# The first batch's attention as one hand-written list, with weight conversions at a fixed pace

## The chip, the cores and the metric

The program runs on one core of a Trainium2 chip. Its engines are TensorE (PE; PEld is its weight load), VectorE (DVE), ScalarE (ACT), GpSimd (POOL) and SyncE (SP), which issues nearly all transfers. The metric is the device time of one execution in microseconds.

## What is computed

Nystrom attention over 8 batches of 8 heads (576 tokens, 64 wide), and two feed-forward layers behind it:

```python
q_lm = q.reshape(B, H, 32, 18, 64).mean(axis=3)        # landmarks; k_lm the same
A, Bm, C = sm(q, k_lm), sm(q_lm, k_lm), sm(q_lm, k)    # sm: scaled softmax
Z = Bm.T / (norm1(Bm) * norminf(Bm) + 1e-6)
for _ in range(6): Z = 2 * Z - Z @ Bm @ Z
x = (A @ Z @ C @ v)                                    # 4608 x 512
x = relu(x @ w_in) ** 2 @ w_out                        # w_in 512 x 2048
...                                                    # then top-1 of 8 experts, 512 x 1024 x 512
```

The two layers' weights w_in and w_out arrive as 64-bit floats and are turned into 32-bit floats on the chip. A product is kept exact enough by splitting each operand in a high and a low part and summing three products.

## The kernel before

**Stages.** A *prologue* does batch 0's attention and converts the first weights. Then, for each batch b, `gemm(b)` makes two passes c = 0, 1 over 288 tokens each. A pass runs over 16 slices f of the hidden width: six matmuls make `hp` from `gb` (the product G of the attention's small factor `wt` with w_in, in rounds n of 512 columns, rows 4n to 4n+3 of f) and `ab` (the transposed A); ACT makes `r` (relu) and `gh`, `g2` (squares), DVE `gl`; twelve matmuls of `second` add the slice to four banks `acc` with w_out's parts `wo`, two slices later. From batch 1 on, G is made from the converted w_in that has been written to memory (`win_d`) and is read back as `wi`. The attention of batch b+1 is a generator of steps (`unit`); `point`, four times a slice, takes steps at `RATES[b, c]`. After batch 7 the experts' stage follows.

**Conversion.** `convert` handles 32 pieces of 128 x 512, first the 16 of w_in, then the 16 of w_out: a transfer `raw` (four buffers), a cast of the high half (`m`, on ACT or POOL), a scaled copy of the low half (`r`, ACT), and two additions on POOL (`halves`) into `wf` (w_in) or `w` (w_out). `wo` takes a high part (ACT) and a low part (DVE). In the prologue pieces are taken by a count (`CONV_SOON`, `CONV`), later on four of five ticks.

**What sets the order.** The framework's list scheduler places the instructions of each engine from priorities (`high_priority`) and dependencies; `follow(a, b)` ties a behind b. In the prologue the attention's steps have high priority, and `sooner` gives a further one to the chain that ends in `wt`: landmarks, softmax of B (`mb`, `bc`), its powers (`ee`, `ef`, six rounds of a matmul and a copy), values, `wz`, `wt`. Beside it runs A: scores, exponentials (`aa`), `at`, `ab`. Win_d's stores and the loads of batch 1's q and k go out in the prologue as buffers come free.

## Time and profile before

| | us |
|---|---|
| median of 3 runs | 1259.39 (1259.34 to 1260.92) |
| profiled execution | 1259.2 |
| its span in the trace | 1257.5 |
| PE busy | 1206.7 (96%) |
| ACT, DVE, POOL busy | 615.2, 591.3, 421.3 |
| mean granted TensorE clock | 0.978 of full |

The span is what the trace covers, from the first instruction to the last. A busy PE is one with a matmul in flight; its clock has two levels, 1.2 and 2.4 GHz, and the granted clock of a stretch is the mean share of the upper one.

### The profile page before, as it was taken

The numbers are of one execution on the slowest core, as the hardware profiler recorded it, in microseconds if no ns is written. First come the engines' busy times: TensorE is split into PE (matmuls) and PEld (weight loads), VectorE is DVE, ScalarE is ACT, GpSimd is POOL, SyncE is SP. The second block draws the span as 40 slices with busy tenths as digits, with TensorE's granted clock in tenths as the row PEclk, the third lists the DMA queues.
The fourth block names the chain that finished last, engine by engine and source line by source line (L and its number), as shares of the span: only waits on it lengthen the run. The fifth ranks groups of instructions, "written<-read, shape, count | busy, mean of one in ns | idle before, by whom it ended". The sixth has DMA issues, their size and how long they took to land.

```text
span 1257.5 us, 25149 instructions
## 1 busy us (share of the span) xinstructions
PE 1206.7 (96%) x9834; PEld 1078.6 (86%) x9834; DVE 591.3 (47%) x1498; ACT 615.2 (49%) x1433; POOL 421.3 (34%) x568
## 2 busy tenths in 40 slices
PE   4598999999999999999999999999999999999996
PEld 3377888989989989989989999998888888888885
DVE  5586466567547557556556332233333323323231
ACT  5586364564564564564564454553343433424331
POOL 5787514332233233232112000163342423424220
PEclk7699999999999999999999999999999999999998
DMA  9944333252152142141133210152534435343231
GB/s 339 336 164 135 124 122 109 91 168 61 59 171 64 53 158 77 53 158 58 54 120 108 69 37 2 39 151 84 143 105 139 129 115 159 108 125 110 90 96 40
DMA packets 88408, 142.24 MB, mean 113 GB/s; under 512 B 6430, under 2 KB 61758, under 8 KB 84702
## 3 DMA queue, kind: packets, MB, share of 16 engines
q1 hardware_dynamic: 87854, 139.97, 34.4%
q8 instruction: 79, 1.29, 0.4%
q0 software_dynamic: 288, 0.43, 0.1%
q14 instruction: 43, 0.35, 0.1%
q10 hardware_dynamic: 144, 0.20, 0.0%
HBM read 117.47 MB, written 23.11 MB: 112 GB/s over the span
## 4 chain that ended last, share of the span: by engine, by line
PE 90%; DVE 3%; DMA 3%; ACT 2%; POOL 1%; issue 1%; SPq 0%; POOLq 0%; ACTq 0%; DVEq 0%
PE acc L402 32%; PE hp L402 32%; PE y L402 17%; PE two L398 4%; PE bank L398 2%; PE bank L410 1%; DMA raw<-in_moe_w_in_dram 1%; PE pl L398 1%; DMA v<-in_v_dram 1%; PE pt L1168 1%; DVE x L488 1%; DMA t<-in_q_dram 1%; DVE gl L1079 1%; ACT r L185 0%; DVE ma L559 0%
## 5 line engine op out<-in xcount | busy, mean ns | idle before, releaser
L402 PE MATMUL acc<-gh,wo 128*128 128x288 f32 x2048 | 453.5, 299 | 7.7 <-ACT wo L218 5.0
L402 PEld LDWEIGHTS acc<-gh,wo 128*128 128x128 f32 x2048 | 341.1, 189 | 30.0 <-ACT gh L1077 8.4
L402 PE MATMUL acc<-gl,wo 128*128 128x288 f32 x1024 | 288.9, 298 | 1.1 <-DVE gl L1079 1.1
L402 PE MATMUL hp<-ab,gb 128*128 128x288 f32 x1536 | 255.7, 301 | 1.6 <-ACT r L1076 1.5
L402 PEld LDWEIGHTS hp<-ab,gb 128*128 128x128 f32 x1536 | 216.0, 189 | 21.3 <-issue 11.8
L1076 ACT ACTIVATE r<-hp 128x288 f32<-128x288 f32 x256 | 105.4, 412 | 256.0 <-PE hp L402 254.4
L1079 DVE TENSOR_TENSOR gl<-g,gh 128x288 fp32r<-128x288 f32 x256 | 131.4, 514 | 198.8 <-ACT g L1078 192.6
L402 PE MATMUL y<-s,h 128*128 128x512 f32 (+1 forms) x896 | 223.0, 396 | 0.8 <-ACT h L1311 0.5
L402 PEld LDWEIGHTS hp<-xs,s 128*128 128x128 f32 x1536 | 212.2, 188 | 7.5 <-DVE ls L1522 0.3
L402 PE MATMUL hp<-xs,s 128*128 128x288 f32 x1536 | 217.1, 295 | 0.2 <-DVE ls L1522 0.2
L402 PEld LDWEIGHTS acc<-gl,wo 128*128 128x128 f32 x1024 | 193.4, 189 | 4.0 <-DVE gl L1079 3.0
L402 PEld LDWEIGHTS y<-s,h 128*128 128x128 f32 (+1 forms) x896 | 160.6, 184 | 37.7 <-ACT h L1311 0.7
L230 POOL TENSOR_TENSOR s<-r,s 128x256 fp32r<-128x256 f32 x128 | 102.0, 819 | 234.8 <-ACT s L218 234.8
L1311 ACT ACTIVATE h<-hp 128x288 fp32r<-128x288 f32 x128 | 52.6, 412 | 186.8 <-PE hp L402 172.6
L1314 DVE SCALAR_TENSOR_TENSOR h<-hp,h 128x64 fp32r<-128x64 f32 (+2 forms) x192 | 62.6, 354 | 166.3 <-ACT h L1311 165.9
L1077 ACT ACTIVATE gh<-r 128x288 fp32r<-128x288 f32 x256 | 114.2, 446 | 12.5 <-PE acc L402 5.8
L1078 ACT ACTIVATE g<-r 128x288 f32<-128x288 f32 x256 | 110.6, 432 | 5.3 <-DVE gl L1079 5.0
L218 ACT CAST s<-r 128x512 fp32r<-128x512 f32 x128 | 77.6, 617 | 71.4 <-PE y L402 56.1
L499 POOL COPY x<-x 32x576 f32<-32x576 f32 x48 | 33.9, 706 | 195.7 <-DVE x L488 102.7
L224 DVE TENSOR_TENSOR s<-r,s 128x512 fp32r<-128x512 f32 x64 | 50.9, 795 | 103.3 <-ACT s L218 103.3
L230 POOL TENSOR_TENSOR xs<-xr,xs 128x576 fp32r<-128x576 f32 x32 | 45.9, 1459 | 64.0 <-ACT xs L218 48.0
L444 POOL TENSOR_TENSOR st<-t 128x288 f32<-128x288 f32 x50 | 40.7, 835 | 75.1 <-DMA t<-in_q_dram 73.1
(198 smaller groups left out, 1097.7 us busy)
## 6 DMA issues: line engine op xcount, KB each, us to landing
r<-in_moe_w_dram SPq DMA_DIRECT2D x128, 256.0 KB
wi<-win SPq DMA_DIRECT2D x28, 1024.0 KB
t<-in_k_dram SPq DMA_DIRECT2D x16, 576.0 KB
t<-in_q_dram SPq DMA_DIRECT2D x16, 576.0 KB
v<-in_v_dram SPq DMA_DIRECT2D x32, 288.0 KB
x_d<-x SPq DMA_DIRECT2D x16, 576.0 KB
xr<-x_d SPq DMA_DIRECT2D x16, 576.0 KB
raw<-in_moe_w_in_dram SPq DMA_DIRECT2D x16, 511.8 KB
```

The costliest lines, as they stand in the source:

```text
L218: hi = self.nc.scalar.copy(out=t[:, 0], in_=raw)
L224: lo_eng.tensor_tensor(out=t[:, 1], in0=raw, in1=t[:, 0].bitcast(F32), op=ALU.subtract)
L230: self.nc.gpsimd.tensor_tensor(out=out[:, p], in0=in0[:, p], in1=in1[:, p], op=op)
L398: self.in_run(lambda: self.nc.tensor.matmul(out, **kw))
L402: mm = self.nc.tensor.matmul(out, **kw)
L444: add = lambda out, in0, in1: self.nc.gpsimd.tensor_tensor(out=out, in0=in0, in1=in1, op=ALU.add)
L1076: nc.scalar.activation(out=r, in_=hp[:, 0:HC], func=ACTF.Relu)
L1077: nc.scalar.activation(out=gh, in_=r, func=ACTF.Square)
L1078: nc.scalar.activation(out=g2, in_=r, func=ACTF.Square)
L1079: nc.vector.tensor_tensor(out=gl, in0=g2, in1=gh.bitcast(F32), op=ALU.subtract)
L1311: nc.scalar.activation(out=h[:, t0:t1], in_=hp[:, 0:HC], func=ACTF.Relu)
L1314: nc.vector.scalar_tensor_tensor(out=h[:, to + a:to + z], in0=hp[:, a - t0:z - t0], scalar=0.0, in1=h[:, a:z].bitcast(F32), op0=ALU.max, o ...
```

## The change

The generator of batch 0's attention gives way to one list in `prologue`. While `strict` is true, the wrapper `Lanes` ties each instruction behind the one that was written before it on the same engine, SP's transfers too. This lasts until rounds 0 and 1 of G are out. The list interleaves the attention with `cv()`, a step of the conversion. Three pieces of w_out follow the first eight of w_in, then both alternate. In the list, odd pieces from 5 on are cast on ACT and the rest on POOL; afterwards odd ones on POOL and even ones on DVE. In the pass (0, 0) each slice takes two steps of conversion (`CONV = 2.0`), releases two held stores of w_in and, at three slices, sums of batch 1's landmarks. Rounds 2 and 3 of G come at slices 6 and 10. DVE takes over one of the squares in that pass, all sums of batch 0 and 1, and batch 0's half of the products with 1/sum. Batch 1's loads and stores into `win_d` move behind the list, its attention steps come slower, and its G rounds later (`G_LATER`).

```diff
-CONV_BUFS = 2
+CONV_BUFS = 3
+CONV = 2.0
+SUMS_AT = {3: ("k", 0), 5: ("k", 1), 7: ("q", 0)}
+OUT_AHEAD = 3
+FIRST_G = (6, 10)
-RATES = {(0, 0): 0.3, (0, 1): 0.8}
+RATES = {(0, 0): 0.2, (0, 1): 0.65}
-G_STEPS = {7: 0, 10: 1, 13: 2, 15: 3}
+G_STEPS = {(1, 7): 0, (1, 10): 1, (1, 13): 2, (1, 15): 3}
+G_LATER = {(1, 15): 0, (2, 2): 1, (2, 6): 2, (2, 10): 3}
...
+    def in_lane(self, name, op):
+        if self.strict is not None and hasattr(op, "ins"):
+            if name in self.lanes:
+                self.follow(op, self.lanes[name])
+            if self.strict:
+                self.lanes[name] = op
+        return op
...
-            if i < 4 * KD and i % 2 == 0:
-                nc.scalar.activation(out=top, in_=high, func=ACTF.Copy)
+            ops = []
+            if self.strict and i > 4 and i % 2:
+                ops.append(nc.scalar.activation(out=top, in_=high, func=ACTF.Copy))
+            elif self.strict or i % 2:
+                ops.append(nc.gpsimd.tensor_copy(out=top, in_=high))
             else:
-                nc.gpsimd.tensor_copy(out=top, in_=high)
+                ops.append(nc.vector.tensor_copy(out=top, in_=high))
...
+    def weights_order(self):
+        i, o = self.convert_in(), self.convert_out()
+        first, rest = i[:G_FIRST * KD], i[G_FIRST * KD:]
+        jobs = first + o[:OUT_AHEAD]
+        for k, w in enumerate(rest):
+            jobs += [w, o[OUT_AHEAD + k]]
+        return jobs + o[OUT_AHEAD + len(rest):]
+    def split_out(self, last):
+        while len(self.wo) <= min(last, NFC - 1):
+            f = len(self.wo)
+            while f not in self.whole:
+                next(self.conv)
+            while self.g_done <= f // KD:
+                self.first_g_of(self.g_done)
+            w = self.whole[f]
...
+            self.nc.scalar.copy(out=hi, in_=w)
+            self.nc.vector.tensor_tensor(out=lo, in0=w, in1=hi.bitcast(F32), op=ALU.subtract)
...
+    def convert_on(self, f):
+        self.due_conv += CONV
+        while self.due_conv >= 1.0:
+            self.due_conv -= 1.0
+            next(self.conv, None)
+        if f > 0:
+            self.release(2)
+        if f in SUMS_AT:
+            self.sums(self.ahead, *SUMS_AT[f])
...
-        work = self.unit(u)
-        while True:
-            with self.tc.high_priority(URGENT):
-                got = next(work, None)
...
+        self.strict = True
+        cv()
+        for nm, hg in (("k", 0), ("k", 1), ("q", 0), ("q", 1)):
+            self.sums(u, nm, hg)
+        for nm, hg in (("k", 0), ("k", 1), ("q", 0)):
+            for i in range(3):
+                self.transposed(u, nm, hg, i)
+        self.landmarks(u, "k")
+        for i in range(3):
+            self.transposed(u, "q", 1, i)
+        cv()
+        self.scores_a(u, 0)
+        cv()
+        self.scores_a(u, 1)
+        self.landmarks(u, "q")
+        cv()
...
+        self.last_values(u)
+        self.weights(u)
+        next(a0, None)
+        for _ in range(3):
+            next(a1, None)
+        cv(2)
...
-                    nc.scalar.activation(out=g2, in_=r, func=ACTF.Square)
+                    if (b, c) == (0, 0):
+                        nc.vector.tensor_tensor(out=g2, in0=r, in1=r, op=ALU.mult)
+                    else:
+                        nc.scalar.activation(out=g2, in_=r, func=ACTF.Square)
```

DVE's order in the prologue, from the sums of batch 0 (`sums`) to the second power of B (`ee`, `ef`), before:

```order
L455 TENSOR_REDUCE sums<-t 128x32 x6
L588 TENSOR_REDUCE mc<-bank 128x1
L616 TENSOR_REDUCE mb<-bank 128x2
L588 TENSOR_REDUCE mc<-bank 128x1
L617 TENSOR_SCALAR mb<-mb 128x2
L592 TENSOR_SCALAR mc<-mc 128x1
L626 TENSOR_SCALAR mb<-mb 128x2
```

And of the change, where every line of the list reads L103, the wrapper's:

```order
L103 TENSOR_REDUCE sums<-t 128x32 x8
L103 STREAM_TRANSPOSE aa<-two 128x9x32 x2
L103 STREAM_TRANSPOSE aa<-bank 128x9x32 x2
L103 TENSOR_REDUCE mb<-bank 128x2
L103 TENSOR_SCALAR mb<-mb 128x2
L103 TENSOR_REDUCE ma<-aa 128x18
L103 TENSOR_SCALAR mb<-mb 128x2
```

Two more sums and the scores of A (`aa`) now stand ahead of B's softmax; the maxima of C (`mc`), which stood among it, come later.

PE's order at the end of batch 0's second pass, around the last steps of batch 1's inverse (`bank<-eu,dg`), `wz` and round 0 of batch 1's G (`two<-wi,wt`), before:

```order
L402 MATMUL acc<-gl,wo 128x288
L402 MATMUL acc<-gh,wo 128x288
L402 MATMUL hp<-ab,gb 128x288 x6
L402 MATMUL acc<-gh,wo 128x288 x4
L398 MATMUL two<-wi,wt 32x512 x8
L410 MATMUL bank<-ident,sums 128x128 x2
L402 MATMUL acc<-gl,wo 128x288
L402 MATMUL acc<-gh,wo 128x288
```

And of the change (L455, L459 and L467 are the helpers that record small matmuls, large ones and transposes):

```order
L459 MATMUL acc<-gl,hi 128x288
L459 MATMUL acc<-gh,lo 128x288
L455 MATMUL bank<-eu,dg 128x96 x2
L455 MATMUL bank<-eu,dg 128x64 x2
L467 MATMUL bank<-ident,wz 128x128
L455 MATMUL two<-wi,wt 32x512 x8
L467 MATMUL bank<-ident,sums 128x128
L459 MATMUL hp<-ab,gb 128x288 x6
```

Before, 55 of the pass's 192 `acc` matmuls are still to come when G goes out (the last inverse step and `wz` stand two slices and one slice above); now all 192 stand ahead of the last two inverse steps, and the next `hp` is batch 1's first.

## Rows read from the trace of the kernel before

**Rows 1.** Windows: PE, PEld, DVE, ACT, POOL busy us, PE clock, DMA share, GB/s.

```profile
0.00:55.80 55.80, 29.94 (x488) 17.87 (x489) 27.52 (x91) 31.07 (x62) 37.55 (x62) 0.66 1.00 348
55.80:131.00 75.20, 62.46 (x571) 53.11 (x563) 57.07 (x101) 54.75 (x129) 60.83 (x82) 0.95 0.48 164
131.00:1246.00 1115.00, 1112.67 (x8778) 1006.58 (x8778) 504.98 (x1305) 528.00 (x1243) 319.97 (x420) 1.00 0.31 98
```

**Rows 2.** Timeline of PE around the first GEMM: start, us, instruction, idle before.

```profile
50.71 3.67 PE L398 MATMUL bank<-wf,wt 64*32 64x512 f32 x32 [0.89 <-ACT wt L816]
...
55.80 0.40 PE L402 MATMUL hp<-ab,gb 128*128 128x288 f32 x1
...
61.03 0.90 PE L410 MATMUL bank<-ident,t 128*128 128x128 f32 x3 [3.60 <-ACT x L473]
```

**Rows 3.** Timeline of ACT at the end of the first pass.

```profile
130.64 0.76 ACT L1115 COPY x<-acc 128x288 f32<-128x288 f32 x2 [1.92 <-PE acc L402]
```

**Rows 4.** Timeline of DVE in the prologue.

```profile
4.63 6.36 DVE L455 TENSOR_REDUCE sums<-t 128x32 f32<-128x576 f32 x6 [0.34 <-DMA t<-in_k_dram]
```

**Rows 5.** Groups by form, 0 to 140 us: busy, mean ns | idle.

```profile
L230 POOL TENSOR_TENSOR wf<-m,r 128x256 int32<-128x256 int32 x32 | 22.5, 728 | 8.7 <-ACT r L185 8.3
...
L562 DVE TENSOR_TENSOR aa<-aa,ma 128x576 f32<-128x576 f32 x2 | 1.5, 752 | 0.0
```

**Rows 6.** Timeline of ACT in the prologue.

```profile
53.42 0.67 ACT L218 CAST ab<-at 128x576 fp32r<-128x576 f32 x1 [2.38 <-DVE at L823]
53.99 2.04 ACT L1019 CAST gb<-bank 128x512 fp32r<-128x512 f32 x4
```

**Rows 7.** Groups by line and form, 55.8 to 131 us.

```profile
L230 POOL TENSOR_TENSOR w<-m,r 128x256 int32<-128x256 int32 x32 | 25.0, 805 | 6.8 <-DVE wo L224 6.8
...
L184 POOL CAST m<-raw 128x512 f16<-128x512 bf16 x16 | 14.1, 902 | 0.1
L224 DVE TENSOR_TENSOR wo<-w,wo 128x512 fp32r<-128x512 f32 x16 | 13.2, 827 | 9.0 <-ACT wo L218 9.0
...
L1079 DVE TENSOR_TENSOR gl<-g,gh 128x288 fp32r<-128x288 f32 x18 | 11.6, 645 | 5.4 <-ACT gh L1077 3.6 <-ACT g L1078 1.6
...
L1078 ACT ACTIVATE g<-r 128x288 f32<-128x288 f32 x20 | 8.9, 444 | 4.2 <-DVE gl L1079 3.9
L455 DVE TENSOR_REDUCE sums<-t 128x32 f32<-128x576 f32 x8 | 8.8, 1158 | 0.1
...
L1020 DVE TENSOR_TENSOR gb<-two,gb 128x512 fp32r<-128x512 f32 x4 | 2.7, 682 | 0.1
```

**Rows 8.** DMA issues, 0 to 140 us: xcount, KB each.

```profile
raw<-in_moe_w_in_dram SPq DMA_DIRECT2D x16, 511.8 KB
...
win<-wf SPq DMA_DIRECT2D x16, 256.0 KB
t<-in_k_dram SPq DMA_DIRECT2D x7, 576.0 KB
```

**Rows 9.** Page, part 5: the same operation over the whole kernel.

```profile
L1079 DVE TENSOR_TENSOR gl<-g,gh 128x288 fp32r<-128x288 f32 x256 | 131.4, 514 | 198.8 <-ACT g L1078 192.6
```

**Rows 10.** Chain that ended last, first GEMM: start, us, what.

```profile
66.82 0.79 PE hp L402 x6
```

**Rows 11.** Windows of PE's instructions that write the tile bank.

```profile
55.80:131.00 75.20, 11.47 (x165) 0.95 0.48 164
```

**Rows 12.** Windows of PE's instructions that write the tile two.

```profile
55.80:131.00 75.20, 4.69 (x88) 0.95 0.48 164
```

**Rows 13.** Timeline of PE, batch 1's last inverse step to its G.

```profile
155.11 0.55 PE L398 MATMUL bank<-eu,dg 128*128 128x64 f32 x4
...
160.50 1.09 PE L398 MATMUL two<-wi,wt 64*32 64x512 f32 x16
```

**Rows 14.** Timeline of DVE over the same steps.

```profile
152.90 0.42 DVE L806 TENSOR_TENSOR dg<-bank,h 128x256 f32<-128x256 f32 x1 [1.71 <-PE bank L398]
...
155.70 1.17 DVE L712 TENSOR_TENSOR wz<-eu,bank 32x128 f32<-32x128 f32 x4 [1.68 <-PE bank L398]
```

More of the change, by code (lines that the diff above doesn't have):

```diff
@@ L90, in weave, with __init__, __getattr__, call @@
                 yield got
+class Lane:
+    def __init__(self, kernel, name, engine):
+        self.kernel, self.name, self.engine = kernel, name, engine
+    def __getattr__(self, what):
+        fn = getattr(self.engine, what)
+        if not callable(fn):
+            return fn
+        def call(*args, **kw):
+            return self.kernel.in_lane(self.name, fn(*args, **kw))
+        return call
+class Lanes:
+    NAMES = ("tensor", "vector", "scalar", "gpsimd", "sync")
+    def __init__(self, kernel, nc):
+        self.nc = nc
+        for name in self.NAMES:
+            setattr(self, name, Lane(kernel, name, getattr(nc, name)))
+    def __getattr__(self, what):
+        return getattr(self.nc, what)
 class Kernel:
     def __init__(self, tc, ins, out):
-        self.tc, self.nc, self.out = tc, tc.nc, out
+        self.tc, self.nc, self.out = tc, Lanes(self, tc.nc), out
+        self.lanes, self.strict, self.due_conv = {}, None, 0.0
         self.q, self.k, self.v, self.w_in, self.w_out, self.w_gate, self.w_og, self.w1, self.w2 = ins
@@ L115, in hold, with tick @@
             self.held.append(fn)
-    def tick(self, convert=True):
+    def tick(self):
         self.now += 1
-        if convert and self.conv is not None and self.now % CONV_TICKS:
-            next(self.conv, None)
         run = [e for e in self.later if e[0] <= self.now]
@@ L296, in run @@
             self.first_g()
-            for _ in range(CONV_FIRST):
-                next(self.conv)
             self.pend = []
@@ L560, in softmax_a @@
         most = ma[:, 0].unsqueeze(2).to_broadcast(wide)
-        if u["early"]:
-            nc.vector.tensor_tensor(out=af, in0=af, in1=most, op=ALU.subtract)
-        else:
-            self.halves(af, af, most, ALU.subtract)
+        self.halves(af, af, most, ALU.subtract)
         nc.scalar.activation(out=af, in_=af, func=ACTF.Exp, scale=SCALE / SEG)
@@ L854, in cv @@
         def cv():
-            if not u["early"]:
-                yield from self.softmax_b(u)
+            yield from self.softmax_b(u)
             for j in range(2):
@@ L936, in prologue, with cv @@
         self.constants()
-        conv = self.conv = self.convert(self.convert_in() + self.convert_out())
-        next(conv)
+        conv = self.conv = self.convert(self.weights_order())
+        u = self.unit_of(0, early)
+        self.ahead = self.unit_of(1)
+        self.strict = True
+        def cv(n=1):
+            for _ in range(n):
+                next(conv)
+        cv()
[4 more added lines that the diff above has]
+                self.transposed(u, nm, hg, i)
@@ L955, in prologue @@
-        self.drain()
+        sb = self.softmax_b(u)
+        next(sb)
+        for i in range(2):
+            self.scores_c(u, i)
+        a0, a1 = self.exp_a(u, 0), self.exp_a(u, 1)
+        next(a0)
+        next(sb)
+        next(sb)
+        pw = self.powers(u)
+        next(pw)
+        cv(2)
+        self.exp_c(u, 0)
+        next(pw)
+        cv()
+        self.exp_c(u, 1)
+        next(pw)
+        self.transposed_c(u, 0)
+        next(a0)
+        next(pw)
+        cv()
+        next(a1)
@@ L957, in first_g @@
+        next(pw)
+        for j in (1, 2):
+            self.transposed_c(u, j)
+        next(a1)
+        self.norm_c(u)
+        next(pw)
+        cv()
+        self.values(u, 0)
+        for _ in range(2):
+            next(a0)
+        next(pw)
+        next(pw, None)
+        self.values(u, 1)
+        self.first_values(u)
+        cv()
+        self.last_values(u)
[3 more added lines that the diff above has]
+            next(a1, None)
+        cv(2)
     def first_g(self):
@@ L964, in first_g @@
             self.drain()
-        held, self.held = self.held, None
-        for fn in held:
-            fn()
+        self.strict = False
         self.banks = [self.aux]
+        for _ in range(3):
+            self.load_next()
     def chunk(self, b, n, rows):
@@ L986, in chunk @@
                     )
+                    if self.last_h is not None and self.lead is self.last_pe:
+                        self.follow(self.lead, self.last_h)
         self.gt[b, n] = self.gb.tile([128, 2, 2, 512], F32R, tag="gb", name="gb")
@@ L1025, in all_steps @@
         for b in range(1, B):
-            yield from self.unit(self.unit_of(b))
+            yield from self.unit(self.ahead if b == 1 else self.unit_of(b))
     def load_at(self, b, c):
@@ L1039, in follow, with release @@
         )
+    def release(self, n):
+        for _ in range(min(n, len(self.held))):
+            self.held.pop(0)()
+    def convert_on(self, f):
[7 more added lines that the diff above has]
+            self.sums(self.ahead, *SUMS_AT[f])
     def behind(self, mm):
@@ L1099, in second @@
         nc = self.nc
-        while f not in self.wo:
-            next(self.conv)
+        self.split_out(f)
         if f == 0:
```

222 lines of the change are left out of this document (122 added, 100 removed).

## The prediction

> **What bounds the kernel now.** I read the windows first. From 131 us to 1246 us PE is busy for 1112.67 of 1115 us at full clock [rows 1]: there it is the bound and nothing is to be had. Before 131 us it is not. Up to 55.8 us it is busy for 29.94 us at a mean granted clock of 0.66, and from there to 131 us for 62.46 of 75.2 us [rows 1]. So 38.6 us of idle time, and some half-clock time, lie in the part that the change rewrites. PE's timeline then gives two marks. The G matmuls of batch 0 begin at 50.71 us and the first `hp` at 55.80 us, but PE is held again until 61.03 us, behind ACT [rows 2]. The pass (0, 0) ends where ACT can copy out its banks, at 130.64 us after a wait for PE [rows 3]; I call it 131.0.
>
> So the change is worth what it does to two lengths, the prologue (55.8 us) and the first pass (75.2 us), less what it leaves undone for later. Call H the start of the first `hp` and E the end of the first pass.
>
> **The prologue, H.** DVE is the longest list, so I count that. Before 55.8 us it is busy for 27.52 us [rows 1]. The change adds two sums; six took 6.36 us, so 2.1 us [rows 4]. Two 128x576 operations come over from POOL, one for `aa` and one for `ab`, at 0.75 us each [rows 5]. That makes 31.1 us, and a floor near 32 us, since DVE starts at once. To this I add three waits in which the list gives DVE nothing else. Between the last sum and B's softmax lie a landmark product, a copy, another product and an exponential: 5 us, an estimate; in it DVE can still transpose the scores of A. The six rounds of powers each go to PE and back; the list fills most gaps with `aa` and `mc`, and I take 3 us. At the end `ab`'s cast (0.67 us) and one cast of G (2.04 us for four) stand on ACT ahead of DVE's last pieces [rows 6]: 1.2 us. H = 0.9 (its start) + 31.1 + 9.2 = 41 us. Lower bound 36 (half of these waits), upper 50: the order is now fixed, so a late transfer or ACT's queue holds everything behind it.
>
> POOL must have eight pieces of w_in ready: 16 additions of 0.728 us [rows 5], seven casts of at most 0.902 us [rows 7] and two halves of `aa`, 19.5 us in all, which DVE's 41 us cover if the first raw piece is there by 15 us. Transfers: q, k and v of batch 0 and fourteen raw pieces are 10.6 MB [rows 8], at the 348 GB/s of the prologue [rows 1] 30 us. Neither sets H.
>
> **The first pass, E.** No engine was saturated in it before; PE waited for `wo` and `gl` in turn. I add up each engine's list for the new pass.
> - DVE: 16 `gl` at 0.645, 16 new squares (no such row; between ACT's 0.444 for the same square and `gl`'s 0.645; I take the latter, the same engine and shape), 16 low parts of `wo` at 0.827, 10 casts (between DVE's 0.682 for 128x512 and POOL's 0.902; I take 0.68), 6 sums at 1.158, 4 parts of G at 0.682 [rows 7], and some 3 us of batch 1's softmax: 53 us. With the low prices 46.
> - POOL: 21 pieces of two additions at 0.805, 11 casts at 0.902 [rows 7], `ab`: 45 us. It loses batch 2's sums and `halves` in this stretch.
> - ACT: 54.75 us before [rows 1], without 20 squares of 0.444 [rows 7], with a few more pieces: 48 us.
> - PE: 62.46 us before, less what is now left for later (next part): 53 us.
> - Transfers: 19 raw pieces of 511.8 KB, 16 stores of 256 KB, five loads of 576 KB and one v [rows 8]: 17 MB, 49 us at 348 GB/s.
>
> Five lists between 45 and 53 us. They can't interlock perfectly; DVE's 53 us, 1.7 us until its first `gl`, and 1.3 us for the last slice give 56 us. E = 41 + 56 = 97 us, against 131.0. Bounds for the pass: 47 us and the old 75.2 us.
>
> The price of the squares is the open one. `gl` takes 0.514 us over the whole kernel [rows 9] and 0.645 us in the first pass [rows 7], where POOL is busy for 60.83 of 75.2 us [rows 1]. At 0.514 the squares would cost 2.1 us less and E would be 95 us. The Trainium skill (GPSIMD Engine Reference, section 1) says that POOL shares its SBUF interfaces with DVE and contends with DVE instructions that have two SBUF inputs; the squares are such, and by that rule they take the higher price. The two rows of `gl` agree with it.
>
> **What is left for later.** At 131.0 us the kernel before had five slices of `hp` of the second pass out; by the order of the change there will be two. Three slices at 0.79 us are 2.4 us [rows 10]. Batch 1's attention costs PE 11.47 + 4.69 us in that stretch, some 1.1 us of it G [rows 11, 12]; by the order, a quarter of the transposes, all matmuls of `ec` and of the values, and half of the scores remain: about 7 us of it (between 5 and 10). So the time saved is 131.0 - 9.4 - E: with E = 97, 24.6 us.
>
> **The wait that comes instead.** At the end of batch 0's second pass PE's order now has all `acc` matmuls ahead of the last two inverse steps, `wz`, G and the first `hp` of batch 1. That is a chain without cover. An inverse step takes 0.55 us on PE and, with `dg` at 0.42 us and two smaller copies, 0.75 on DVE; the last one 0.55 us and `wz` 1.17 us; transpose and copy of `wt`, 0.6 us (estimate); half of the 1.09 us of two rounds of G; then a cast and the low part, 0.51 + 0.51 + 0.68 us [rows 6, 7, 13, 14]. Together 5.9 us. Round 1 of that G stands directly ahead of slice 4, with the pass drained again: 0.55 + 1.7 = 2.2 us. After such gaps PE runs a while at half clock, as it does up to 55.8 us; 1 us. Total 9 us, between 3 and 13.
>
> **Sum.** 1257.5 - 24.6 + 9 = 1241.9 us of span. The profiled execution took 1259.2 us for 1257.5 us of span, and lies at the median (1259.39). So 1243.6; I say 1244 us.
>
> **Rivals.**
> - The pass is starved. If conversions come in the fixed order but as slowly as before, the pass still takes 75.2 us: E = 116, saved 5.6 us, minus 9: 1262.6 us, slower. For it: three engines, PE and the transfers have nearly equal lists, SP's order is strict over raw pieces, stores and loads, and only four raw buffers exist. Against: POOL lost batch 2's work, the first three pieces of w_out are ready when the pass starts. It decides from a pass of 72 us on.
> - The wait at the batch's end is covered, because PE reaches it later than the order suggests or batch 1's chain is early: 1235 us. Against it, the order itself: nothing stands between.
> - The list does not shorten the prologue much: ACT carries the copies of q and k, exponentials and casts in one order, and a raw piece that comes late holds all. H = 50: 1253 us.
>
> **How the numbers follow.** I give the forecast 0.58, the covered wait 0.17, the long prologue 0.15, the starved pass 0.10. A change of less than 0.2% (2.5 us) could hardly be told from none. The first two and most of the third are faster: 0.83. The edge of the third and of the fourth is no change: 0.07. Slower: 0.10. The range goes from E = 89 with a cheaper end of batch (1232) to a prologue of 50 us with a slightly longer pass (1257).
>
> **What would show it.** Right: first `hp` near 41 us; ACT's copy out of `acc` near 97 us; a PE gap of 5 to 6 us just ahead of batch 1's first `hp`; DVE busy over nine tenths in the pass. Wrong: `hp` after 48 us, with DVE or PE waiting for ACT; a pass over 65 us with PE waiting for `hi` or `lo` and POOL for raw; or new idle time of PE after the first two batches, where I expect none.

## The result, and the profile after

The changed kernel takes 1269.82 us (median of 4 runs, 1268.21 to 1271.27) against 1260.16 us for the kernel before (4 runs, 1259.34 to 1261.89): ratio 1.0075, 95% interval 1.0057 to 1.0092. It is slower by 0.75%, where 1244 us were forecast. The profiled execution took 1268.21 us for a span of 1266.1 us.

The windows of the changed kernel come first, cut at its own marks (first `hp`, end of the first pass, end of batch 0, 190 us). The columns are those of [rows 1].

```profile
0.00:40.32 40.32, 25.27 (x481) 17.28 (x481) 32.22 (x89) 24.74 (x53) 26.09 (x42) 0.80 0.83 273
40.32:108.20 67.88, 56.40 (x416) 47.29 (x417) 58.17 (x101) 45.91 (x103) 47.73 (x57) 0.92 0.82 283
108.20:156.00 47.80, 47.21 (x459) 43.77 (x458) 23.63 (x53) 22.50 (x57) 12.47 (x18) 1.00 0.25 78
156.00:190.00 34.00, 26.53 (x208) 19.62 (x207) 17.07 (x67) 13.19 (x34) 12.25 (x20) 0.77 0.28 98
190.00:1246.00 1056.00, 1052.63 (x8248) 949.15 (x8247) 474.81 (x1212) 501.49 (x1166) 307.22 (x405) 1.00 0.31 98
```

The prologue and the first pass together are 22.8 us shorter than in [rows 1] (108.20 against 131.00 us). The fourth line is new: for 34 us behind the end of batch 0 PE is busy for 26.53 us only, at a mean granted clock of 0.77, where the kernel before loses nothing in the 34 us behind its own end of batch 0:

```profile
175.03:209.03 34.00, 34.00 (x379) 29.41 (x378) 20.41 (x57) 19.11 (x49) 11.93 (x18) 1.00 0.39 133
```

The marks themselves, first in PE's timeline and then in ACT's; they answer to [rows 2] and [rows 3].

```profile
36.07 3.67 PE L103 MATMUL bank<-wf,wt 64*32 64x512 f32 x32 [0.45 <-ACT wt L103]
...
40.32 0.85 PE L103 MATMUL hp<-ab,gb 128*128 128x288 f32 x2 [0.59 <-ACT gb L103]
```

```profile
108.16 0.70 ACT L1278 COPY x<-acc 128x288 f32<-128x288 f32 x2
...
155.93 0.93 ACT L1278 COPY x<-acc 128x288 f32<-128x288 f32 x2 [1.48 <-PE acc L459]
```

The first `hp` comes at 40.32 us instead of 55.80, the end of the first pass at 108.16 us instead of 130.64, the end of batch 0 at 155.93 us instead of 175.03: up to there the change leads by 19.1 us. Then it gives all of it back. ACT's first relu of batch 1 is 6.0 us ahead (167.64 against 173.69 us), that of batch 1's second pass 0.6 us (224.35 against 224.91 us), and the last copy of `acc` in batch 7 is 8.5 us behind (842.35 against 833.85 us); from there to the end both take 423.7 us. PE's timeline of the changed kernel shows two places in between where PE waits:

```profile
158.72 0.63 PE L455 MATMUL bank<-eu,dg 128*128 128x64 f32 x4 [1.47 <-DVE eu L839]
160.70 0.44 PE L467 MATMUL bank<-ident,wz 128*128 128x128 f32 x1 [1.36 <-DVE wz L820]
161.50 1.96 PE L455 MATMUL two<-wi,wt 64*32 64x512 f32 x16 [0.35 <-ACT wt L925]
165.55 2.06 PE L459 MATMUL hp<-ab,gb 128*128 128x288 f32 x6 [1.67 <-ACT gb L1154]
...
174.34 0.96 PE L459 MATMUL hp<-ab,gb 128*128 128x288 f32 x6
...
183.12 0.22 PE L1366 MATMUL pc<-x,ones 128*32 128x32 f32 x2 [0.82 <-DVE m L1355]
...
185.17 2.06 PE L459 MATMUL hp<-ab,gb 128*128 128x288 f32 x6 [1.07 <-ACT gb L1154]
```

The first four rows are the uncovered chain: last inverse step, `wz`, round 0 of G, first `hp` of batch 1, each behind a wait. At 183.12 us PE waits for DVE's `m` of the experts' choice for batch 0, whose counts (`pc`) stand in PE's order between round 1 of G, at 181.21 us, and the `hp` that needs it; the last row is that `hp`. At both places six `hp` take 2.06 us instead of the 0.96 us of the row at 174.34 us, and the granted clock of the windows 160 to 170 and 180 to 190 us is 0.52 and 0.71, where 0.5 is the lower of the two levels throughout:

```profile
150.00:160.00 10.00, 7.87 (x60) 7.49 (x59) 8.34 (x26) 2.57 (x7) 5.11 (x9) 1.00 0.26 87
160.00:170.00 10.00, 6.82 (x33) 4.01 (x34) 3.07 (x6) 3.52 (x9) 8.95 (x16) 0.52 0.55 196
170.00:180.00 10.00, 10.00 (x89) 8.91 (x88) 2.47 (x7) 5.03 (x12) 2.19 (x4) 0.97 0.01 2
180.00:190.00 10.00, 7.83 (x76) 5.21 (x76) 8.20 (x43) 3.91 (x12) 0.00 (x0) 0.71 0.31 105
```

### The profile page after: what moved, and what is told of

It is laid out like the page before. It is cut to its first block, busy times and chain, and to the rows that moved or that the text cites. A ratio compares the mean times of both kernels' runs of the same rounds, so it can differ in the third digit from the quotient of the medians.

```text
span 1266.1 us, 25177 instructions
## 1 busy us (share of the span) xinstructions
PE 1218.2 (96%) x9858; PEld 1085.4 (86%) x9858; DVE 609.0 (48%) x1524; ACT 610.7 (48%) x1414; POOL 408.8 (32%) x547
## 4 chain that ended last, share of the span: by engine, by line
PE 88%; DVE 7%; POOL 2%; issue 1%; ACT 1%; DMA 1%; POOLq 0%; DVEq 0%; ACTq 0%
PE hp L459 31%; PE acc L459 29%; PE y L459 16%; PE two L455 3%; PE bank L455 2%; PE bank L103 1%; PE bank L467 1%; DVE x L554 1%; PE pl L455 1%; DVE lo L103 1%; DMA raw<-in_moe_w_in_dram 1%; PE pt L1331 1%; DVE mb L103 1%; DVE gl L103 0%; DVE ma L657 0%
## 5 line engine op out<-in xcount | busy, mean ns | idle before, releaser
L459 PE MATMUL acc<-gl,hi 128*128 128x288 f32 x964 | 270.0, 297 | 2.1 <-DVE gl L1237 1.5
L459 PE MATMUL acc<-gh,lo 128*128 128x288 f32 x964 | 268.8, 296 | 0.0
L459 PE MATMUL hp<-ab,gb 128*128 128x288 f32 x1434 | 242.3, 304 | 3.4 <-ACT gb L1154 2.7
L1237 DVE TENSOR_TENSOR gl<-g,gh 128x288 fp32r<-128x288 f32 x224 | 114.0, 510 | 238.2 <-ACT g L1236 236.6
L459 PEld LDWEIGHTS hp<-ab,gb 128*128 128x128 f32 x1434 | 203.2, 190 | 25.4 <-issue 12.4
L459 PE MATMUL y<-s,h 128*128 128x512 f32 (+1 forms) x896 | 223.0, 396 | 0.8 <-ACT h L1474 0.5
L459 PEld LDWEIGHTS hp<-xs,s 128*128 128x128 f32 x1536 | 212.2, 188 | 7.5 <-DVE ls L1685 0.3
L459 PE MATMUL hp<-xs,s 128*128 128x288 f32 x1536 | 217.1, 295 | 0.2 <-DVE ls L1685 0.2
L1231 ACT ACTIVATE r<-hp 128x288 f32<-128x288 f32 x224 | 91.9, 410 | 228.5 <-PE hp L459 227.9
L459 PE MATMUL acc<-gh,hi 128*128 128x288 f32 x964 | 200.1, 301 | 0.0
L459 PEld LDWEIGHTS y<-s,h 128*128 128x128 f32 (+1 forms) x896 | 160.6, 184 | 37.7 <-ACT h L1474 0.7
L459 PEld LDWEIGHTS acc<-gl,hi 128*128 128x128 f32 x964 | 181.5, 188 | 7.1 <-DVE gl L1237 2.6
L459 PEld LDWEIGHTS acc<-gh,lo 128*128 128x128 f32 x964 | 181.1, 188 | 1.4 <-issue 1.4
L459 PEld LDWEIGHTS acc<-gh,hi 128*128 128x128 f32 x964 | 150.6, 189 | 18.4 <-ACT gh L1232 12.6
L1232 ACT ACTIVATE gh<-r 128x288 fp32r<-128x288 f32 x224 | 99.5, 444 | 8.2 <-PE acc L459 1.7
L1236 ACT ACTIVATE g<-r 128x288 f32<-128x288 f32 x224 | 96.0, 429 | 0.5 <-DVE gl L1237 0.5
```

The costliest lines, as they stand in the source:

```text
L459: mm = self.nc.tensor.matmul(out, **kw)
L1231: nc.scalar.activation(out=r, in_=hp[:, 0:HC], func=ACTF.Relu)
L1232: nc.scalar.activation(out=gh, in_=r, func=ACTF.Square)
L1236: nc.scalar.activation(out=g2, in_=r, func=ACTF.Square)
L1237: nc.vector.tensor_tensor(out=gl, in0=g2, in1=gh.bitcast(F32), op=ALU.subtract)
```

## The experiments

All ratios are to the kernel before, on the same chip. "Old tables" means RATES and G_LATER as before the change; the kernel with them is the base of most runs.

### The two tables

Both tables old, everything else as changed:

```
-RATES = {(0, 0): 0.2, (0, 1): 0.65}
+RATES = {(0, 0): 0.3, (0, 1): 0.8}
-G_LATER = {(1, 15): 0, (2, 2): 1, (2, 6): 2, (2, 10): 3}
+G_LATER = G_STEPS
```

> The changed kernel, with the two tables that set batch 1's attention and its G (RATES, G_LATER) as before the change. In the profiles the change is 19.1 us ahead of the kernel before at the end of batch 0's second pass (ACT's last copy of acc, 175.03 against 155.93 us), 6.0 us ahead at batch 1's first relu, 0.6 us ahead at its second pass (224.91 against 224.35 us), and then falls behind by a further 9 us until batch 7. Theory J (junction: the tables leave batch 1's inverse, wz and G to stand uncovered at the end of batch 0): without them PE does not wait at the end of batch 0; batch 1's first relu comes near 158 us instead of 167.64 and the second pass near 214 us; about 10 us faster than the change, 1258 to 1261 us in time if the later loss stays. Theory L (the later loss of 9 us comes from the phase of the attention that these tables set): then that goes too, about 1250 us. Theory S (first pass starved of converted weights by a fixed order of transfers): the first pass ends at 108 us or later as in the change, since it gets more attention to do (some 7 us), 112 to 116 us, and what J gains is paid here; time 1266 to 1270 us.

Measured: 1248.03 us, ratio 0.9907 (0.9891 to 0.9924), as J and L together had it. So the rest of the change makes the kernel 12 us faster, and the two tables cost the change 21.8 us. The first pass ends at 112.22 us, 4 us later than in the change, since it carries more of batch 1's attention; batch 1's first relu comes at 162.09 us, its second pass at 212.15 us, the last copy at 822.09 us. The windows of this kernel from 112.2 us on:

```profile
112.20:156.00 43.80, 43.36 (x435) 39.25 (x433) 26.36 (x65) 20.74 (x52) 18.71 (x27) 1.00 0.22 68
156.00:190.00 34.00, 34.00 (x363) 29.35 (x356) 22.57 (x55) 23.44 (x58) 11.37 (x18) 1.00 0.59 190
```

Where the changed kernel lost 7.5 us of PE time and some clock, PE is busy for 34.00 of 34 us at full clock. Its lead over the kernel before is 18.4 us at the end of the first pass, some of it attention left for the second, and steady from there: 11.8 us at the end of batch 0, 11.6 and 12.8 us at batch 1's two passes, 11.8 us at the last copy.

The same two tables alone, put into the kernel before:

> The kernel before, with only the two tables RATES and G_LATER of the change. Theory J: the prologue and the first pass stay as they were but the pass loses some 7 us of attention, so it can end no more than 7 us earlier than 130.64 us; at the end of batch 0 there is an uncovered chain of some 9 to 12 us as in the change; time 1262 to 1270 us, 3 to 10 us above the kernel before. Theory L: the dense part after 225 us also grows by 9 us, as it does in the change: 1270 to 1278 us. If neither holds, the time is that of the kernel before within 3 us.

Measured: 1268.41 us, ratio 1.0078 (1.0051 to 1.0104). They cost 8.4 us there too, without any of the change's other parts. In the traces 4.0 us of it are there when batch 1's second pass begins (228.89 against 224.91 us), and the stretch from there to the last copy takes 5.7 us more, so both J and L have a part. Then one table at a time, in the changed kernel. With the slow RATES and G at the old places:

```
-G_LATER = {(1, 15): 0, (2, 2): 1, (2, 6): 2, (2, 10): 3}
+G_LATER = G_STEPS
```

> The changed kernel with its slow RATES kept and the rounds of G at the old places (G_LATER as G_STEPS). With both tables old the kernel took 1248.03 us, with both new 1269.82 us. Theory R (the slow RATES alone cost it: they leave batch 1's attention behind, so that its inverse and wz stand behind the last acc of batch 0 whatever the places of G): in the order wz still stands at the end of batch 0, so PE waits there as in the change, 8 us and more; 1262 to 1270 us. Theory G (the late places of G cost it): 1248 to 1254 us.

Measured: 1263.57 us, ratio 1.0029 (1.0018 to 1.0041), as theory R had it. With the old RATES and the late G:

```
-RATES = {(0, 0): 0.2, (0, 1): 0.65}
+RATES = {(0, 0): 0.3, (0, 1): 0.8}
```

> The changed kernel with the old RATES, and the late places of G kept. Theory R: batch 1's inverse and wz are done within batch 0's second pass (wz 12 hundredths of a pass ahead of its end, as with both old); only round 0 of G and its split stand uncovered, 1.09 / 2 + 1.7 us, and half clock behind it: 1249 to 1253 us. Theory G: 1262 to 1270 us.

Measured: 1265.64 us, ratio 1.0046 (1.0032 to 1.0060). Theory R fell here: the late G alone costs 17.6 us, nearly as much as both. PE's timeline of this kernel tells why:

```profile
163.35 0.33 PE L467 MATMUL bank<-ident,sums 128*128 128x128 f32 x1 [2.33 <-POOL sums L509]
...
167.25 1.21 PE L455 MATMUL two<-x,lm 64*32 64x288 f32 x16 [2.08 <-DVE mc L685]
174.13 1.09 PE L467 MATMUL bank<-ident,ec 128*96 128x128 f32 x4 [5.67 <-ACT ec L692]
175.15 1.96 PE L455 MATMUL two<-wi,wt 64*32 64x512 f32 x16
```

`wz` was done in time, but the steps of batch 2's attention (`sums`, `lm`, `ec`) are written ahead of the late G and stand ahead of it in PE's order, and they wait for POOL, DVE and ACT with no large product left to cover them. The two tables are no sum of two costs: each alone leaves an uncovered chain at the end of batch 0, batch 1's own or batch 2's.

Slow only in the first pass, all G early (on old tables):

```
-RATES = {(0, 0): 0.3, (0, 1): 0.8}
+RATES = {(0, 0): 0.2, (0, 1): 0.9}
```

> The kernel of the first experiment (1248.03 us, steps of batch 1's attention at 0.3 a point in the first pass and 0.8 in the second), with 0.2 and 0.9: the first pass carries as little of the attention as in the change, the second more, and in the order wz stands at 1.88 passes as with 0.3 and 0.8, with all of G at the old places. Theory Q (what counts is that wz and G are out before the last acc of batch 0, not how slow the first pass goes): no wait at the end of batch 0, the first pass ends up to 4 us earlier, time 1244 to 1250 us. Theory R (the slow first pass itself leaves batch 1 late, whatever follows): 1256 us and more.

Measured: 1266.01 us, ratio 1.0044 (1.0027 to 1.0062). Theory Q fell. The order has `wz` at the same place, but the second pass has to carry what the first left: it ends 60.8 us behind the end of the first (51.0 us with 0.3 and 0.8), and PE is busy for 6.85 of 10 us from 140 us on, where DVE is busy for 9.49.

### The loss behind 225 us

From batch 1's second pass to the last copy the change takes 618.0 us, the kernel before 608.9, the kernel with old tables 609.9. Two runs went at it. The first lets the loads and POOL's sums run free once the conversions are over:

```
-        if self.last_h is not None or self.last_gb is not None or self.pacer is not None:
+        if self.conv is not None and (self.last_h is not None or self.last_gb is not None or self.pacer is not None):
...
-                self.paced(add(x[:, c:c + n], t[:, c:c + n], t[:, 2 * n + c:3 * n + c]))
+                add(x[:, c:c + n], t[:, c:c + n], t[:, 2 * n + c:3 * n + c])
```

> The changed kernel, where the loads of later batches, and POOL's partial sums, are no longer tied behind the last hp once the conversions are over; the first batches stay as in the change. Theory P (the loss of 9 us between 225 and 842 us is from those ties: PE's small matmuls on the sums stand alone 20 times where they stood in 10 groups, and are inserted one by one among the large ones): the later loss shrinks to 0 to 3 us, time 1261 to 1264 us. Theory L (the loss is from the phase in which the attention starts, set by the tables): no change, 1268 to 1271 us. The milestones up to 225 us stay within 1 us of the change in both.

Measured: 1270.85 us, ratio 1.0090 (1.0073 to 1.0107), no change: theory P fell; the stretch takes 619.6 us. Its marks up to there were to be those of the change and are not (the first pass ends at 112.90 us, batch 1's second pass begins at 220.44 us), so the stretch says more here than the total. The second lets batch 1's attention catch up:

```
-RATES = {(0, 0): 0.2, (0, 1): 0.65}
+RATES = {(0, 0): 0.2, (0, 1): 0.65, (1, 0): 0.6, (1, 1): 0.6}
```

> The changed kernel, with 0.6 steps a point in batch 1 (0.4 there and from then on in the change): the attention that the slow RATES leave behind is caught up within batch 1, and the lag of half a pass that stands in the order of every later batch (wz at 5.50 passes against 5.00) falls to a quarter and less. Theory W (the 9 us that the change loses behind 225 us are mostly that deferred work itself, PE time that has to be paid somewhere): it is paid in batch 1 instead, the second pass of batch 1 begins later than 224 us, and the end moves by at most 3 us: 1266 to 1270 us. Theory L (the lag costs anew in every batch): the loss of 9 us is gone, 1259 to 1262 us.

Measured: 1270.40 us, ratio 1.0088 (1.0068 to 1.0108). The sum came out as theory W said, but not for its reason. From the seventh pass (batch 3's first) to the last copy this kernel takes 462.4 us, the change 471.4, the one with old tables 463.7: where the lag is gone, the loss is gone, as L had it. It was paid before: from batch 1's first relu to the seventh pass it takes 214.4 us, the change 203.3, the one with old tables 196.4, with PE waiting again (32.70 us busy in the 44 us from 156 us). And W's deferred work does not exist. The windows of all PE work from batch 1's second pass to the last copy, the change first, then the kernel with old tables:

```profile
224.35:842.35 618.00, 615.76 (x5500) 561.02 (x5501) 324.70 (x867) 335.27 (x838) 165.47 (x246) 1.00 0.25 85
```

```profile
212.15:822.09 609.94, 608.03 (x5500) 558.31 (x5501) 330.84 (x868) 331.85 (x838) 168.62 (x247) 1.00 0.27 86
```

The same 5500 matmuls at full clock keep PE busy for 7.7 us longer. By tile, those that write `two` take 43.76 us against 40.58 us (704 in both), `hp` and `bank` differ by 0.2 us and `acc` by 1.2 us the other way. Of the tile `two`, the rounds of G take 26.1 us in both, the products with the landmarks (`two<-x,lm`) 17.6 against 14.4 us. In the change five of their twenty groups of 16 are cut in a piece of 4 and one of 12, 5.5 to 7.2 us apart, and each piece keeps PE busy about as long as a whole group:

```profile
293.00 0.68 PE L455 MATMUL two<-x,lm 64*32 64x288 f32 x4 [0.18 <-DVE x L558]
...
300.20 0.70 PE L455 MATMUL two<-x,lm 64*32 64x288 f32 x12
...
316.66 0.72 PE L455 MATMUL two<-x,lm 64*32 64x288 f32 x16
```

Five such cuts make up the 3.2 us. So the lag changes which small groups stand together; where the rest of the 7.7 us goes stays open.

The runs of the single tables show which of them does it. The same stretch takes 607.2 us with only G late, 614.7 us with only RATES slow and 616.4 us with 0.2 and 0.9. So the loss goes with RATES and not with G's places; those cost at the end of batch 0, where batch 1's first relu comes 18.7 us later than with old tables (180.83 against 162.09 us).

### The list

On old tables, the ties of the list taken out, and the same program order kept; the scheduler orders the prologue:

```
-        if self.strict is not None and hasattr(op, "ins"):
+        if False and self.strict is not None and hasattr(op, "ins"):
```

> The kernel of the first experiment (the change with both tables old, 1248.03 us), written in the same order but without the ties of each operation behind the one before it on its engine; the scheduler orders the prologue. Theory T (the ties make the short prologue): first hp at 44 us or later instead of 39 to 40 us, time 1251 to 1258 us. Theory U (the shorter prologue comes from the other edits of the first batch, the squares, sums and conversions on other engines, and the order follows by itself): first hp within 2 us, time 1246 to 1250 us.

Measured: 1258.38 us, ratio 0.9985 (0.9976 to 0.9995). Theory T: the ties are worth 10.35 of the 12 us. The first `hp` comes at 44.98 us (39.26 with ties), the first pass takes 74.1 us from first relu to last copy (70.2). Of the 16.5 us by which the first `hp` comes earlier than in the kernel before, 10.8 come without the ties, so U holds for most of the prologue itself.

### The first pass

It took 67.8 us where 56 were forecast. First the three loads of batch 1, which stand on SP's queue ahead of the raw pieces (base: the change):

```
-        for _ in range(3):
-            self.load_next()
...
+        if f < 3:
+            self.load_next()
```

> The changed kernel, with batch 1's first three loads (k, k, q, 576 KB each) issued one each in slices 0, 1 and 2 of the first pass, not all three at the end of the prologue ahead of the raw pieces. Theory S (the raw pieces stand behind these loads on SP's queue, and the pass waits for hi and lo): the three loads are 1.7 MB, 5 us at 350 GB/s, so raw pieces come up to 5 us earlier, the gaps of PE before hi at 76 to 98 us (1.35, 2.04, 0.73 us and others) shrink and the pass ends at 103 to 105 us instead of 108.16. Since the junction waits for batch 1's chain, the total moves by less: 0 to -4 us against the change. Theory not S (conversions themselves set the pace, POOL and DVE full): the pass ends at 108 us, no change within 1 us, or a loss of 1 to 2 us where the sums of batch 1 wait for their loads.

Measured: 1275.89 us, ratio 1.0130 (1.0113 to 1.0147). Theory S fell: the pass ends at 113.55 us, 5.4 us later. The raw pieces do not come earlier: the next one behind these loads is issued at 42.72 us, and at 42.39 us in the change. In the pass PE waits 7.4 us for `hi` (1.7 us in the change), and ACT 10.9 us for POOL's additions ahead of it (4.8 us); what starts this is not shown. The next ones are on old tables, where the pass takes 70.2 us from first relu to last copy. The squares back on ACT (there is no pass (9, 9), so the second branch is always taken):

```
-                    if (b, c) == (0, 0):
+                    if (b, c) == (9, 9):
                         nc.vector.tensor_tensor(out=g2, in0=r, in1=r, op=ALU.mult)
                     else:
```

> The kernel of the first experiment (the change with both tables old, 1248.03 us), with the 16 squares of the first pass on ACT as before the change. In the profile of the change a square takes DVE 0.45 us where POOL is idle and 0.8 to 1.0 us where POOL adds, 16 of them some 11 us of a pass of 67 us. Theory D (DVE's list sets the first pass, as the prediction had it): the pass (first relu to the last copy of acc, 42.03 to 112.22 us) shortens by 5 to 10 us, time 1239 to 1244 us. Theory C (the loop sets it: a slice's low part waits for POOL's addition, that for DVE's cast, and the cast stands in DVE's list behind the slice before): a square moves from one link to another, the pass within 2 us, time 1246 to 1250 us. Theory A (ACT then is the late one, since r of the pieces and hi stand in its list): the pass 2 to 6 us longer, 1250 to 1254 us.

Measured: 1245.15 us, ratio 0.9882 (0.9865 to 0.9898): the fastest version here, 1.2% below the kernel before, though its interval overlaps that of the kernel with old tables. But DVE gave up 16 squares of 0.644 us, 10.3 us in all, and the pass shortened by 3.0 us, less than theory D had and more than C. Three pieces a slice (`CONV = 3.0`):

> The kernel of the first experiment (1248.03 us), with three pieces converted a slice of the first pass instead of two (CONV), so that the steps of a piece stand earlier in every engine's list. Theory C (the loop between the slices and the pieces sets the pass): the waits of POOL for DVE's casts, 0.8 to 2.4 us each, go, low parts come earlier, the pass is 4 to 10 us shorter, 1238 to 1245 us. Theory D (an engine's list is the bound, whatever its order): within 2 us of 1248. A third way: the first slices wait behind the pieces that now stand ahead of them, the pass is longer, 1250 to 1256 us.

Measured: 1249.95 us, ratio 0.9919 (0.9903 to 0.9936), pass 71.1 us: theory C fell. POOL's casts of the pass on ACT:

```
-            if self.strict and i > 4 and i % 2:
+            if i % 2 and (i > 4 or not self.strict):
```

> The kernel of the first experiment (1248.03 us), with POOL's casts of the first pass (every second piece, 0.77 to 1.06 us each, some 10 of them) on ACT. Theory P (POOL's list is what the low parts wait for: it is busy for 46 of 60 us there and late): the pass is 3 to 8 us shorter, 1240 to 1246 us. Theory C (the loop): what POOL gains it waits for ACT, whose list holds relu, hi and r of the pieces: within 2 us. Theory A (ACT's list, 39 of 60 us, becomes the late one): 1250 to 1254 us.

Measured: 1248.10 us, ratio 0.9898 (0.9882 to 0.9915), pass 69.3 us: theory P fell. POOL's additions replaced by one copy each:

```
-            self.halves(to[j][:, c:c + W].bitcast(I32), m, r, ALU.add)
+            if self.strict is False:
+                self.nc.gpsimd.tensor_copy(out=to[j][:, c:c + W], in_=m.bitcast(F32))
+            else:
+                self.halves(to[j][:, c:c + W].bitcast(I32), m, r, ALU.add)
```

> The kernel of the first experiment (both tables old, 1248.03 us; first pass 42.03 to 112.22 us), where in the first pass POOL copies the upper part of a weight piece (one 128x512 copy, one operand) instead of adding upper and lower part (two 128x256 additions of 0.85 to 0.89 us, two operands): the low bits of these weights are left out. Theory P (POOL's additions are what the pass waits for, by their own time and by slowing DVE's operations from 0.45 to 0.8 and 1.0 us beside them): the mean of DVE's square falls from 0.65 to about 0.5 us, the pass to 56 to 62 us, the time to 1234 to 1241 us. Theory X (transfers or the loop between the lists): the pass stays within 3 us of 70, 1245 to 1250 us.

Measured: 1246.75 us, ratio 0.9903 (0.9881 to 0.9925), pass 69.5 us: theory P fell. In the groups by form of this kernel, 40 to 110 us, POOL's saved time has turned into waiting:

```profile
L103 POOL CAST m<-raw 128x512 f16<-128x512 bf16 x11 | 9.9, 897 | 7.6 <-DMA raw<-in_moe_w_in_dram 5.7 <-DMA raw<-in_moe_w_out_dram 1.9
L103 POOL COPY w<-m 128x512 f32<-128x512 f32 x13 | 8.7, 683 | 20.4 <-DVE m L103 20.3
```

It waits 20.3 us for DVE's casts and 7.6 us for raw pieces. SP's queue waits too; its waits in the changed kernel, 30 to 105 us (total, times, longest):

```profile
SPq L103 <- ACT r L103: 17.6, 11, 2.8
SPq L103 <- DVE m L103: 12.1, 7, 2.8
```

SP issues a raw load when ACT and DVE have read the buffer that it takes. So I changed the number of raw buffers, to three (`CONV_AHEAD = 3`):

> The kernel of the first experiment (1248.03 us, first pass 70.2 us), with three raw buffers instead of four (CONV_AHEAD). Theory B (a loop of raw buffers sets the pass: load, cast and r in DVE's and ACT's lists, next load): with three quarters of the pieces under way the pass grows by 8 to 20 us, 1254 to 1268 us, and the prologue too. Theory X (the transfers' rate sets it, 17 MB in the pass): no growth beyond 3 us, 1247 to 1251 us.

Measured: 1256.73 us, ratio 0.9976 (0.9966 to 0.9986), pass 74.6 us. Five of them, with two buffers each for `m` and `r`, and these two alone:

> The kernel of the first experiment with five raw buffers, and two instead of three buffers each for m and r (CONV_BUFS), since the memory holds no more. To be compared with the next run, which has the two alone. Theory B: the pass is 5 to 10 us shorter than there. Theory X: the same within 2 us.

> The kernel of the first experiment with two instead of three buffers each for m and r, four raw buffers kept. A piece's cast and r then wait for POOL's addition of the piece before the last. If that is the loop that counts (theory M), the pass grows by 4 to 12 us, 1252 to 1260 us; else it stays within 2 us, 1247 to 1250 us.

Measured: 1250.72 us (0.9929; 0.9912 to 0.9946), pass 69.1 us, and 1251.73 us (0.9936; 0.9919 to 0.9952), pass 71.8 us. One raw buffer less costs 4.4 us of the pass, one more gives 2.6 us, and the buffers of `m` and `r` 1.6 us: the loop of raw buffers has a part in it, but less than theory B had, and theory M fell. Each of these passes is read from one trace.

### The chain at the end of batch 0, and one more step

Is the chain late because DVE is crowded? In the change, without the low parts of the second pass:

```
-                    nc.vector.tensor_tensor(out=gl, in0=g2, in1=gh.bitcast(F32), op=ALU.subtract)
+                    if (b, c) != (0, 1):
+                        nc.vector.tensor_tensor(out=gl, in0=g2, in1=gh.bitcast(F32), op=ALU.subtract)
+                    else:
+                        gl = gh
```

> The changed kernel (1269.82 us), without DVE's 16 low parts (gl) in the second pass of batch 0; the products take the high part in their place, so that PE's work is the same and the low part of that pass is left out. It takes some 9 us off DVE's list between 108 and 156 us, some 3 us of it in the crowded 140 to 156 us. Theory V (DVE's crowded list makes batch 1's softmax and inverse late): the wait of PE between the last acc of batch 0 and batch 1's first hp (first relu 11.7 us behind the last copy of acc) shrinks to 5 to 8 us, the time by 4 to 8 us to 1262 to 1266 us. Theory K (the chain of the inverse itself, DVE to PE and back, is that long whatever else DVE does): the wait stays within 1.5 us, 1267 to 1271 us.

Measured: 1269.20 us, ratio 1.0074 (1.0057 to 1.0091). PE's timeline of this kernel:

```profile
160.70 0.45 PE L467 MATMUL bank<-ident,wz 128*128 128x128 f32 x1 [1.36 <-DVE wz L820]
...
165.55 2.06 PE L459 MATMUL hp<-ab,gb 128*128 128x288 f32 x6 [1.68 <-ACT gb L1154]
```

The two rows stand at the same microsecond as in the change. Theory K: what is left of the chain when PE runs dry is as long as it is. Last, the fastest version with 0.9 instead of 0.8 in the second pass:

> The kernel with the squares on ACT (1245.15 us), with batch 1's attention at 0.9 steps a point in the second pass instead of 0.8; in the order wz comes a fifteenth of a pass earlier. With nothing to wait for at the end of batch 0 any more (PE idle for less than 1 us between 150 and 180 us in the kernel of the first experiment) theory Q expects no change, 1244 to 1247 us. If the denser second pass makes PE wait for DVE, as 0.2 and 0.9 did (PE 3 us idle in 140 to 150 us), 1248 to 1256 us.

Measured: 1252.22 us, ratio 0.9930 (0.9914 to 0.9947): 7 us slower. The trace is of the slowest of its four executions (1255.98 us). Batch 0 ends in time, at 160.89 us, but batch 1's first pass takes 55.1 us from first relu to first relu, against 50.1 us with 0.8, and the stretch behind it 614.2 against 609.9 us. The time lies in the second range, but not for its reason. PE's one wait in that first pass is for a load, with which the earlier attention seems to have caught up:

```profile
193.02 1.50 PE L455 MATMUL bank<-v,et 96*32 96x64 f32 x48 [2.42 <-DMA v<-in_v_dram]
```

## Why the prediction was wrong

**The prologue, H: right.** 41 us forecast, 40.32 us measured; DVE was busy for 32.22 us of them, where 31.1 us were counted. The ties account for 5.7 us of the gain, by the untied list (44.98 against 39.26 us); most of it comes without them.

**The first pass, E: the DVE sum and the step "They can't interlock perfectly" failed.** The pass took 67.9 us instead of 56. The prediction added 3 us to DVE's list of 53 us; the list was 58.2 us, and DVE was idle for 9.7 us. So the list was 5.2 us too short and the allowance 6.7 us. The price of the squares was right (0.647 us for 0.645), the count of the list was not. DVE's groups of the pass that show it:

```profile
L103 DVE TENSOR_TENSOR g<-r 128x288 f32<-128x288 f32 x16 | 10.4, 647 | 2.0 <-ACT r L103 1.9
L103 DVE TENSOR_REDUCE sums<-t 128x32 f32<-128x576 f32 x8 | 9.2, 1192 | 0.0
L103 DVE TENSOR_TENSOR gb<-two,gb 128x512 fp32r<-128x512 f32 x4 | 2.8, 688 | 1.7 <-ACT gb L103 1.7
L103 DVE TENSOR_TENSOR gb<-bank,gb 128x512 fp32r<-128x512 f32 x4 | 2.5, 683 | 0.0
L103 DVE TENSOR_TENSOR ab<-at,ab 128x576 fp32r<-128x576 f32 x1 | 1.0, 1035 | 0.7 <-ACT ab L103 0.7
```

There are eight sums where six were counted, eight parts of G where four were, a part of `ab`, and batch 1's small operations take some 8 us where 3 were taken. (The groups overlap a little, so they add up to more than 58.2 us.) The other lists came out near: PE 56.4 us (53 forecast), POOL 47.7 (45), ACT 45.9 (48).

What causes the idle time stays open. Six runs that relieved one engine, one pace or one buffer moved the pass by 3 us at most to the better, five of them on old tables. None took transfers out of the pass, though the DMA engines are busy throughout from 40 to 80 us in the change (share 1.01 and 0.95, at 371 and 336 GB/s): that the transfers set that part is untested. From 80 to 100 us every list waits for another (DMA share 0.57, PE 14.91, DVE 16.26, POOL 15.85 of 20 us). That this mixture sets the pass is argued, not shown; shown is that none of the parts that were relieved does alone. E was 108.2 us, not 97: 11.2 us lost.

**Left for later: nearly right.** Four slices of `hp` were left, not three (102 `hp` matmuls by the end of the pass, 126 before, six to a slice). The attention that was named did come in the second pass, transposes 1.5 us, `ec` 1.8, values 1.8, scores 2.1 and 0.6 us more: 7.8 us where 7 were taken. So some 11 us instead of 9.4, and 11.5 us of true gain out of 22.5 us of lead. The kernel with old tables leads by 11.8 us from the end of batch 0 to the last copy.

**The wait that comes instead: too small by some 2 us.** The mechanism was right, PE rows 158.72 to 165.55 us being the chain that the order showed, with gaps of 1.47, 1.36, 0.35 and 1.67 us, 4.9 us, where 5 to 6 us were named. Of the 11.5 us, 6.0 are left at batch 1's first relu, so 5.5 us went there; batch 1's first pass then takes 56.7 us against 51.2, another 5.5 us: 11.0 us for 9. The term most out of size is the half clock, taken at 1 us: by the estimate in the last section it is about 5.6 us. A second one is a misreading: the 16 matmuls of 1.09 us in [rows 13] are one round of G and not two (batch 1's four rounds begin at 161.50, 181.21, 194.97 and 205.97 us, 16 matmuls each), so half of that was too little; at the lower clock the round took 1.96 us.

**"There it is the bound and nothing is to be had": failed.** I took the stretch behind the first two batches as fixed, since PE is busy there all the time. It grew by 9.1 us (618.0 against 608.9 us), with PE busy for 615.8 us of it, so that the sign that I named, new idle time of PE, hardly showed it. A busy PE can take longer over the same matmuls. The slow RATES did it, and some 3 us of it are landmark products cut in two.

The four together: 1241.9 + 11.2 + 1.6 + 2.0 + 9.1 = 1265.8 us; the span is 1266.1 us. None of the rivals is what happened: the starved pass would have needed E = 116, the others were faster. The wait and what lies behind it are 20.1 us; the spans of the change and of the kernel with old tables differ by 20.3 us, their medians by 21.8 us.

## What to carry to other kernels

Where work is moved out of a crowded stretch into a later one, follow it to the point at which its chain has to be done and see what large work still stands beside it there: here the two tables that relieved the first pass cost 21.8 us, more than the 12 us that the rest gained. Two settings that put off two parts of the same chain are not a sum, so each has to be tried alone and with the other. And a PE that is busy all the time is no constant: here its time for the same 5500 matmuls grew by 7.7 us, in part because small groups were cut in two.

## What the runs showed of the hardware

DVE's operations stretch beside POOL's. In the changed kernel a square can take twice as long beside POOL's work as while POOL is idle; DVE's timeline, then POOL's:

```profile
46.07 0.98 DVE L103 TENSOR_TENSOR g<-r 128x288 f32<-128x288 f32 x1
...
59.74 0.45 DVE L103 TENSOR_TENSOR g<-r 128x288 f32<-128x288 f32 x1
```

```profile
44.00 1.85 POOL L103 TENSOR_TENSOR w<-m,r 128x256 int32<-128x256 int32 x2
45.80 1.00 POOL L103 CAST m<-raw 128x512 f16<-128x512 bf16 x1
46.73 1.81 POOL L103 TENSOR_TENSOR w<-m,r 128x256 int32<-128x256 int32 x2
...
60.72 1.93 POOL L103 TENSOR_TENSOR w<-m,r 128x256 int32<-128x256 int32 x2 [2.43 <-DVE m L103]
```

At 46.07 us POOL casts and then adds; at 59.74 us it has been idle since 58.3 us. The five squares of the pass beside which POOL did nothing took 0.45 or 0.46 us each; of the other eleven, eight took longer, up to 1.00 us, and three did not. `lo` (0.68 us alone, up to 1.23) and `gl` (0.45 us alone, up to 1.01) do the same. With POOL's additions replaced by copies the mean of the squares fell from 0.644 to 0.528 us and that of `lo` from 0.920 to 0.823 us, that of `gl` not (0.604 and 0.603 us); POOL's copies still stretch some of them. The rule on shared SBUF interfaces that the prediction named (the Trainium skill, GPSIMD Engine Reference, section 1) agrees with these rows, as all three operations have two inputs in SBUF. But taking part of that contention away gave the pass only 0.7 us.

Gaps of PE cost more than their own length here. In the changed kernel PE is idle for 2.1, 3.2 and 2.2 us in the windows from 150, 160 and 180 us, 7.5 us together. The granted clock is 1.00 in the first of them, 0.52 (nearly all of it at 1.2 GHz) and 0.71 in the other two, and 0.97 from 170 us on, where PE is busy throughout. By an estimate from these rows (6.82 us of busy time x 0.48, 7.83 x 0.29) the lower clock took about 3.3 and 2.3 us more.
